# A strided v load on SyncE, old batches' rows loaded earlier, row scalings apart from their statistics, and a reordered block pair, in attention followed by LayerNorm and a feed-forward layer

## The chip, the cores and the metric

The kernel runs on one core of a Trainium2 chip. Its engines are TensorE (PE; PEld is its weight load), VectorE (DVE), ScalarE (ACT), GpSimd (POOL) and SyncE (SP), which issues transfers (DMAs); ScalarE issues some too. The metric is the device time of one execution in microseconds (us); lower is better.

## The reference

Eight batches of 576 tokens with eight heads of 64. Heads 0 to 3 see the last 32 tokens ("local"), heads 4 to 7 see the earlier tokens of the same residue modulo 32 ("strided"). The result, 512 wide, goes through a LayerNorm and a feed-forward layer of hidden width 2048, and is added to it.

```
rel = pos[:, None] - pos[None, :]
mask_local = (rel >= 0) & (rel < 32)
mask_strided = (rel >= 0) & (pos[None, :] % 32 == pos[:, None] % 32)
scores = where(mask, q @ k.T / 8, -1e9)          # local: heads 0..3, strided: heads 4..7
attn = exp(scores - max);  attn /= attn.sum() + 1e-9
x  = (attn @ v) as [batch, token, 512]
xn = (x - mean(x)) / sqrt(var(x) + 1e-6) * g_ln
out = x + relu(xn @ w_ch1) @ w_ch2
```

## The kernel before

**Tiling.** The feed-forward layer works on nine chunks of 512 tokens: chunk b is the first 512 tokens of batch b, and chunk 8 the last 64 tokens of all eight batches. The hidden width is cut into 16 blocks of 128. For each chunk and block, twelve products make `ph` (hidden before the relu; 4 slices of the model width by 3 products of high and low parts), ScalarE makes `hh` (relu, high part), VectorE makes `hl` (low part), and twelve products add the block to the output sums `po` (4 tiles of 128 tokens by 3). `ph` has one PSUM bank, so the `ph` of a block can begin only when the `hl` of the block before has been read out of it.

**Steps.** The main loop at lines 1359 to 1408 has one step for each chunk and block. A step issues `ph`, `hh` and `hl` of its own block, then the `po` products of the block before. Into the steps are woven: pieces of the attention (`visits`, a generator; heads are treated in pairs, two pairs of each kind to a batch), the weights' preparation, and the residual. TensorE, VectorE, ScalarE, POOL and SyncE each take their instructions in the order in which the program issues them. Attention results go to DRAM (`xdl` for local, `xds` for strided heads) and come back as rows.

**DMAs.** Every DMA that SyncE or ScalarE issues is given one of eight completion semaphores in turn, in the order of the program, and waits until the DMA eight places earlier, whichever engine issued it, has landed.

**The places that the change touches.** (1) `visits` loads the v of the pair two ahead (`load_v`, lines 404 to 419): for the last batches (`by_blocks`) through ScalarE's queue, six DMAs for a strided pair. (2) `coming` (line 1157) prepares, in the steps of chunk 6 (`runs[-1]`), what the last stage needs: the four row tiles of chunk 8 (`late["x8"]`), four row tiles of chunk 7 (two in `late["x"]`, named x, and two later ones, named xs), their normalisation and their transposes (`turn_last`, `turn_seventh`). Its time `at` is the step less 7; a half is the end of a step. (3) `x_normed` (line 785) takes the statistics of some tiles on VectorE, the reciprocal root on POOL, and multiplies the tiles on ScalarE. (4) The last stage, `two_steps` (line 1284), treats chunks 7 and 8 together, a pair of blocks at a time, with seven products of sums in place of eight; `u` and `v` are its PSUM sums, and between them stand the `po` products of the pair before (`waiting`). In the first pair those are the last block of chunk 6, whose output `prev[0].close()` adds to the residual (line 899) and stores.

Row tiles come from a pool of eight buffers (tag `tk`).

Of the kernel before, what the change touches and what calls it, by code (L numbers as in the profile page):

```python
# [12 lines left out]
AF = mybir.ActivationFunctionType  # L13
# [33 lines left out]
def kernel(  # L47
# [10 lines left out]
    nc = tc.nc  # L58

    B, H, S, D = q.shape  # L60
# [12 lines left out]
    NT = CH // P  # L73
# [49 lines left out]
    for jj in range(4):  # L123
        mrow = mask_l[STR * jj:STR * (jj + 1)]
        nc.gpsimd.affine_select(
            out=mrow, in_=mrow, pattern=[[1, 64]], base=-1,
            channel_multiplier=-1, compare_op=ALU.is_ge, fill=FILL)
        nc.gpsimd.affine_select(
            out=mrow, in_=mrow, pattern=[[-1, 64]], base=STR,
# [5 lines left out]
    for c in range(2):  # L135
        for r in range(3):
            msk = mask_s[64 * c:64 * (c + 1), NB * r:NB * (r + 1)]
            nc.gpsimd.affine_select(
                out=msk, in_=msk, pattern=[[-1, NB]], base=-NB * r,
# [619 lines left out]
    def x_load(c, i, t=None, halves=(0, 1)):  # L759

        if t is None:
            t = tkp.tile([P, DM], F32, tag="tk", name=f"x{c}_{i}")
        if c < B:
            parts = [(0, P, c, P * i)]
        else:
            parts = [(REST * j, REST, 2 * i + j, CH) for j in range(2)]
        for p0, n, b, r in parts:
            if 0 in halves:
                nc.sync.dma_start(t[p0:p0 + n, 0:DM // 2], xd_l[b][r:r + n, :])
            if 1 in halves:  # L770
                xs = xd_s[b][0:S].rearrange("(r t) d -> t r d", t=NB)
                nc.sync.dma_start(t[p0:p0 + n, DM // 2:DM], xs[r // STR:(r + n) // STR])
        return t
# [8 lines left out]
        nc.gpsimd.tensor_tensor(out=rs, in0=rs, in1=mhalf, op=ALU.pow)  # L782
        return rs

    def x_normed(name, xs):

        n = len(xs)
        mv = stp.tile([P, NT + 1, 2], F32, tag="mv5", name=f"mv{name}", bufs=1)
        rs = stp.tile([P, NT + 1], F32, tag="rs5", name=f"rs{name}", bufs=2)
        for i, x in enumerate(xs):  # L790
            st = stp.tile([P, 6], F32, tag="st", name=f"st{name}_{i}")
            nc.vector.bn_stats(st, x)
            nc.vector.bn_aggr(mv[:, i], st)
        nc.vector.tensor_scalar(rs[:, 0:n], mv[:, 0:n, 1], 1e-6, None, op0=ALU.add)
        nc.gpsimd.tensor_tensor(
            out=rs[:, 0:n], in0=rs[:, 0:n], in1=mhalf.broadcast_to([P, n]), op=ALU.pow)
        for i, x in enumerate(xs):
            nc.scalar.activation(out=x, in_=x, func=AF.Copy, scale=rs[:, i:i + 1])

    def x_turn(x, name):  # L800
        ps = fresh_bank(f"px{name}").rearrange("p (c x) -> p c x", c=NCC)
# [38 lines left out]
    def ffn2(run, f, h, tiles):  # L840
        for i in tiles:
            products(run.po[i], f, h, i, slice(0, DM), f == run.f0, f == run.f1 - 1)
# [173 lines left out]
    for step in ORDER.split():  # L1016
        what, x = step.split(".", 1)
        n0 = len(tc.nc.cur_bb.bb.instructions)
        if what[0] == "w":
            i = x[2:]  # L1020
# [40 lines left out]
    def visits():  # L1061

        for i in range(2 * NHP - 1, NP):
            p = pairs[i + 1] if i + 1 < NP else None
            pv = pairs[i] if i >= 2 * NHP else None
            scores_and_values(pv, p)
            by_blocks = i >= 3 * NHP
            px = pv if pv and pv.b + 1 < B else None
            if by_blocks:
                spread(px, p)  # L1070
            turned(i + 2)
            if by_blocks:
                yield
            if pv and i + 2 < NP:
                pairs[i + 2].load_v(queue=nc.scalar if by_blocks else nc.sync)
            yield
            (turn_blocks if by_blocks else weights_and_x)(px, p)
            if by_blocks and i + 3 < NP:
                pairs[i + 3].load_half(1, nc.scalar)
            yield  # L1080
# [50 lines left out]
    def turn_seventh(i):  # L1131

        cs = quarter[i]
        px = x_turn(late["x"][i], f"{B - 1}_{i}")
        xh, xl = (t[:, :, cs] for t in x_t(B - 1))
        t1, t2 = (late["ts"][i][:, n] for n in range(2))
        h, l = ([late[n + k][:, :, cs] for n in ("t1", "t2")] for k in "hl")
        nc.scalar.activation(out=xh, in_=px, func=AF.Copy)
        sub(nc.vector, t1, t1, px[:, 0:2])
        sub(nc.vector, t2, t2, t1)  # L1140
        nc.scalar.activation(out=h[0], in_=t1, func=AF.Copy)
        nc.scalar.activation(out=h[1], in_=t2, func=AF.Copy)
        sub(nc.vector, xl, px, raw(xh))
        sub(nc.vector, l[0], t1, raw(h[0]))
        sub(nc.vector, l[1], t2, raw(h[1]))
        sub(nc.vector, t1, t2, px[:, 0:2])
        sub(nc.vector, t2, px[:, 2:4], t2)
# [9 lines left out]
    def coming(f, end):  # L1157

        at = f + 0.5 * end - LAST

        def tiles(n, name):
            return [tkp.tile([P, DM], F32, tag="tk", name=f"{name}_{i}") for i in range(n)]

        if at == -4:
            late["x8"] = tiles(NT, f"x{B}")
            late["x"] = tiles(2, f"x{B - 1}")
        elif at in (-3.5, -2.5, -1.5):
            i = int(at + 3.5)
            x_load(B, i, late["x8"][i])
        elif at == -1:  # L1170
            for i, x in enumerate(late["x"]):
                x_load(B - 1, i + 2, x, (0,))
            x_load(B, NT - 1, late["x8"][NT - 1], (0,))
        elif at == -0.5:
            x_normed("a", late["x8"][0:3])
        elif at == 0.5:
            free_attention()
            x_load(B, NT - 1, late["x8"][NT - 1], (1,))
            for i, x in enumerate(late["x"]):
                x_load(B - 1, i, x, (0, 1) if i < 2 else (1,))  # L1180
        elif at == 2:
            turn_last(0)
            turn_last(1)
        elif at == 3:
            turn_last(2)
        elif at == 3.5:
            x_normed("b", late["x8"][3:] + late["x"])
        elif at == 5:
            turn_last(3)
            turn_seventh(0)  # L1190
        elif at == 5.5:
            turn_seventh(1)
        elif at == 6:
            turn_seventh(2)
            late["s"] = s_forms(0)
        elif at == 7:
            turn_seventh(3)
        elif at == 8:
            more_forms()
# [36 lines left out]
    def seven(po, w, x, start, stop=True):  # L1236

        wh, wl = (t.rearrange("p (c f) -> p c f", c=2) for t in w)
        xh, xl = x
        for c in range(2):  # L1240
            for k, (a, b) in enumerate(((wh, xh), (wh, xl), (wl, xh))):
                nc.tensor.matmul(po, a[:, c], b[:, c, :], start=(start and c + k == 0),  # L1242
                                 stop=(stop and c == 1 and k == 2), skip_group_check=True)
# [40 lines left out]
    def two_steps(p, s, waiting):  # L1284

        f0, f1 = 2 * p, 2 * p + 1
        a = weight_parts(p)
        s = [[x[:, 0], x[:, 1]] for x in s]
        xh, xl = x_t(B - 1)
        b11, b21 = ([t[:, k:k + 2] for t in (xh, xl)] for k in (0, 2))  # L1290
        t1, t2, b22 = ([late[n + k] for k in "hl"] for n in ("t1", "t2", "b22"))
        t3, t4 = ([late[n][:, k:k + 2] for k in (0, 2)] for n in ("t3", "t4"))
        c11 = fresh_bank(f"c11_{p}")
        seven(c11, a[0, 1], b21, True)
        u = fresh_bank(f"u_{p}")
        seven(u, a[0, 0], b11, True)
        p1 = kept(u, f"p1_{p}")
        if p + 1 < NFC // 2:
            coming_s = s_raws(p + 1)
        for work, tiles in waiting[:1]:  # L1300
            ffn2(*work, tiles)
        h0 = h_tiles(f"{B - 1}_{f0}")
        relu_sum(*h0, c11, p1)
        if not two:
            prev[0].close()
            two.append(Seventh())
        v = fresh_bank(f"v_{p}")
        seven(v, s[0], t1, True)
        seven(u, s[1], t2, False)
        p5 = kept(v, f"p5_{p}")  # L1310
        u2 = kept(u, f"u2_{p}")
        for work, tiles in waiting[1:]:
            ffn2(*work, tiles[:NT // 2])
        seven(u, s[2], t3, False)
        seven(v, s[3], b22, False)
        relu_sum(*h_late(f0, f1), u, p5)
        if p + 1 < NFC // 2:
            coming_s = s_parts(*coming_s)
        else:
            coming_s = None  # L1320
            two[0].load()
        for work, tiles in waiting[1:]:
            ffn2(*work, tiles[NT // 2:])
        seven(u, a[1, 1], t4, False)
        hh, hl = h_tiles(f"{B - 1}_{f1}")
        nc.scalar.activation(out=hh, in_=u, func=AF.Relu)
        nc.vector.scalar_tensor_tensor(
            out=hl, in0=u, scalar=0.0, in1=raw(hh), op0=ALU.max, op1=ALU.subtract)
        relu_sum(*h_late(f1, f0), v, u2)
        run = two[0].run  # L1330
        return coming_s, [((run, f0, h0), range(NT)), ((run, f1, (hh, hl)), range(NT))]
# [75 lines left out]
        prev = (r, f, h)  # L1407
        old, new = new, following
    forms = late["s"]
    waiting = [(prev, range(NT))]  # L1410
    fresh.append((ps_h, "h"))
    for p in range(NFC // 2):
        forms, waiting = two_steps(p, forms, waiting)
# [62 lines left out]
```

## Time and profile before

| | us |
|---|---|
| median of three runs | 910.92 (910.90, 910.92, 914.21) |
| profiled execution | 916.03, its span 914.2 |
| TensorE busy in the span | 885.7 (97%) |
| VectorE, ScalarE, POOL busy | 455.6, 241.8, 238.6 |
| TensorE busy in 0 to 60 us | 45.3 of 60 |
| in 60 to 600 us | 540.0 of 540 |
| in 600 to 640 / 640 to 680 us | 37.8 / 40.0 of 40 |
| in 680 to 700 / 700 to 720 us | 16.2 / 16.9 of 20 |
| in 720 to 760 / 760 to 914 us | 39.3 of 40 / 150.3 of 154 |
| granted TensorE clock, mean | 0.987 of full speed |

The span is the time from the first to the last instruction on the core. A busy TensorE is one that has a product in its pipeline, at whatever clock. The granted clock is a share of full speed: 0.5 and 1.0 are its two levels (1.2 and 2.4 GHz). An engine's waits are listed by what ended them; idle time of an engine on which nothing waits costs nothing.

### The profile page before, as it was taken

The page shows a single profiled execution, that of the slowest core. Times are in us where ns is not written, and L with a number is a line of the kernel's source. Part 1 is how long each engine was busy: PE and PEld are TensorE (multiplying, and loading weights), DVE is VectorE, ACT ScalarE, POOL GpSimd, SP SyncE. Part 2 cuts the span into 40 slices and gives each one's busy share as a digit, 9 for nine tenths or more (in the row PEclk, how much of TensorE's full clock was granted, in tenths as well). Part 3 has the DMA queues.
Part 4 walks back from the last instruction along what each step waited for, and adds up shares of the span by engine and source line. Part 5 has one row for each costly group of instructions (what it writes and reads, how often), then busy time and mean ns, then how long its engine had stood idle before and what let it go on. Part 6 is the DMA issues. An engine that isn't in the chain of part 4 may idle for free.

```text
span 914.2 us, 18339 instructions
## 1 busy us (share of the span) xinstructions
PE 885.7 (97%) x7431; PEld 725.0 (79%) x7431; DVE 455.6 (50%) x855; ACT 241.8 (26%) x433; POOL 238.6 (26%) x293
## 2 busy tenths in 40 slices
PE   6699999999999999999999999999998899999998
PEld 4578888888888888888888888887877678888886
DVE  5697475446754455545554464454642573332400
ACT  4566465112211111111111111111112344333200
POOL 6578287110100010001000010001000367676000
PEclk8899999999999999999999999999999999999999
DMA  9989791127795755666575658597732010001210
GB/s 207 204 188 264 168 281 35 21 50 175 141 172 113 125 103 133 120 119 110 117 132 107 121 102 153 110 150 114 143 89 77 7 63 1 1 0 37 81 45 24
DMA packets 330972, 100.64 MB, mean 110 GB/s; under 512 B 269712, under 2 KB 321800, under 8 KB 330888
## 3 DMA queue, kind: packets, MB, share of 16 engines
q1 hardware_dynamic: 258114, 86.11, 42.7%
q10 hardware_dynamic: 72774, 13.36, 9.8%
q8 instruction: 58, 0.95, 0.5%
q14 instruction: 26, 0.21, 0.1%
HBM read 72.37 MB, written 27.06 MB: 109 GB/s over the span
## 4 chain that ended last, share of the span: by engine, by line
PE 87%; issue 5%; DMA 3%; SPq 2%; ACT 2%; DVE 1%; POOL 0%; ACTq 0%; DVEq 0%; POOLq 0%
PE po L837 40%; PE ph L812 30%; PE u L1242 5%; PE sv L659 4%; PE v L1242 2%; PE c L1242 1%; SPq L722 1%; DMA x<-xds 1%; PE px L690 1%; DMA rows<-in_k_dram 1%; PE av L514 1%; PE pp L498 1%; PE av L523 0%; DMA sp<-wd 0%; PE t L377 0%
## 5 line engine op out<-in xcount | busy, mean ns | idle before, releaser
L837 PE MATMUL po<-w,hh 128*128 128x512 f32 x1024 | 320.6, 394 | 0.0
L812 PE MATMUL ph<-xh,w 128*128 128x512 f32 x880 | 294.3, 396 | 9.2 <-DVE hl L823 9.2
L837 PEld LDWEIGHTS po<-w,hh 128*128 128x128 f32 x1024 | 189.1, 188 | 39.6
L823 DVE SCALAR_TENSOR_TENSOR hl<-ph,hh 128x512 fp32r<-128x512 f32 x112 | 77.2, 690 | 282.4 <-ACT hh L818 282.4
L812 PEld LDWEIGHTS ph<-xh,w 128*128 128x128 f32 x880 | 167.4, 190 | 45.6 <-DVE hl L823 10.5
L837 PE MATMUL po<-w,hl 128*128 128x512 f32 x512 | 199.8, 390 | 0.0
L812 PE MATMUL ph<-xl,w 128*128 128x512 f32 x440 | 173.2, 394 | 0.0
L818 ACT ACTIVATE hh<-ph 128x512 fp32r<-128x512 f32 x112 | 66.8, 596 | 338.5 <-PE ph L812 259.7
L488 POOL TENSOR_TENSOR sm<-sm,mx 128x640 f32<-128x640 f32 (+1 forms) x32 | 40.6, 1270 | 350.0 <-issue 201.1
L837 PEld LDWEIGHTS po<-w,hl 128*128 128x128 f32 x512 | 96.1, 188 | 20.7
L812 PEld LDWEIGHTS ph<-xl,w 128*128 128x128 f32 x440 | 83.7, 190 | 17.0
L493 ACT ACTIVATE sm<-sm 128x640 f32<-128x640 f32 (+1 forms) x32 | 23.8, 743 | 104.8 <-POOL sm L488 104.8
L782 POOL TENSOR_TENSOR rs<-rs,mhalf 128x1 f32<-128x1 f32 x28 | 15.3, 550 | 125.2 <-DVE rs L781 90.3
L837 PE MATMUL po<-w,h 128*128 128x512 f32 x186 | 42.3, 389 | 0.0
L1114 POOL TENSOR_TENSOR sr<-sr,w 128x256 f32<-128x256 f32 x48 | 40.2, 838 | 3.8
L837 PEld LDWEIGHTS po<-w,h 128*128 128x128 f32 x186 | 34.9, 188 | 7.2
L1114 POOL TENSOR_TENSOR s<-sr,s 128x256 fp32r<-128x256 f32 x32 | 24.7, 801 | 26.6 <-ACT s L1228 26.6
L239 DVE SCALAR_TENSOR_TENSOR p<-s,p 128x512 uint32<-128x512 uint32 x32 | 22.0, 688 | 11.3 <-ACT p L235 11.2
L484 DVE TENSOR_REDUCE mx<-sm 128x10 f32<-128x640 f32 (+1 forms) x32 | 26.3, 822 | 1.9
L1114 DVE TENSOR_TENSOR x<-po,x 128x512 f32<-128x512 f32 x8 | 5.3, 688 | 39.6 <-PE po L837 29.9
L671 DVE TENSOR_TENSOR xo<-sv,den 128x256 f32<-128x256 f32 (+1 forms) x72 | 24.0, 389 | 0.0
L292 POOL TENSOR_TENSOR w<-r,w 128x512 fp32r<-128x512 f32 x16 | 20.6, 1294 | 8.4 <-ACT w L288 8.3
(193 smaller groups left out, 982.9 us busy)
## 6 DMA issues: line engine op xcount, KB each, us to landing
s<-in_moe_w_ch_dram SPq DMA_DIRECT2D x32, 512.0 KB
out_dram<-x SPq DMA_DIRECT2D x32, 256.0 KB
raw<-in_q_dram SPq DMA_DIRECT2D x104, 72.0 KB
raw<-in_k_dram ACTq DMA_DIRECT2D x68, 72.0 KB
x<-xdl SPq DMA_DIRECT2D x34, 128.0 KB
x<-xds SPq DMA_DIRECT2D x34, 128.0 KB
xdl<-xo SPq DMA_DIRECT2D x16, 256.0 KB
wd<-sm SPq DMA_DIRECT2D x10, 384.0 KB
```

The source lines that it names most:

```text
L239: nc.vector.scalar_tensor_tensor(out=self.p[i], in0=self.bits(i), scalar=3, in1=self.p[i], op0=ALU.logical_shift_left, op1=ALU.bitwise_or)
L484: engine(self.mx[:, :, 0:nt], self.smv, axis=AX.X)
L488: nc.gpsimd.tensor_tensor(out=sm, in0=sm, in1=mx[:, :, 0:nt].unsqueeze(3).broadcast_to([P, 2, nt, w]), op=ALU.subtract)
L493: nc.scalar.activation(out=self.smv, in_=self.smv, func=AF.Exp, scale=SCALE)
L659: nc.tensor.matmul(dst, at, by, start=True, stop=True, tile_position=pos)
L671: nc.vector.tensor_tensor(out=xot[0:n, :, t0:t1], in0=src, in1=pv.den[0:n, :, t0:t1].unsqueeze(3).broadcast_to([n, 2, t1 - t0, D]), op=ALU ...
L812: nc.tensor.matmul(ph, w[:, cc], x[:, cc, :], start=(n + k == 0), stop=(n == NCC - 1 and k == 2))
L818: nc.scalar.activation(out=hh, in_=ph, func=AF.Relu)
L823: nc.vector.scalar_tensor_tensor(out=hl, in0=ph, scalar=0.0, in1=hh.bitcast(F32), op0=ALU.max, op1=ALU.subtract)
L837: nc.tensor.matmul(po, hx[:, cs], w, start=(start and n == 0), stop=(stop and n == 2))
L1114: engine.tensor_tensor(out=out, in0=a, in1=b, op=op)
L1242: nc.tensor.matmul(po, a[:, c], b[:, c, :], start=(start and c + k == 0), stop=(stop and c == 1 and k == 2), skip_group_check=True)
```

## The change

Five edits:

- In one visit, that of pair 27 (`i == NP - 5`), the six v loads of pair 29 go through SyncE's queue instead of ScalarE's.
- The tiles of chunk 8 are taken, and the first three loaded, three steps earlier.
- `x_normed` is cut into `x_stats` (statistics and root) and `x_normed` (scalings). The statistics of the first three tiles move from the end of step 6 to the beginning of step 5, their scalings to the beginning of step 6.
- The statistics of the other five tiles stay at the end of step 10. Their scalings move from there: three to the end of step 11, two to the end of step 12.
- In the first pair of the last stage the `po` products of the last block of chunk 6 are cut in two halves, the second of which goes between the second and third use of `u`; `prev[0].close()` moves behind it, to the end of the pair.

```diff
@@ x_normed
-    def x_normed(name, xs):
+    def x_stats(name, xs):
...
-        for i, x in enumerate(xs):
-            nc.scalar.activation(out=x, in_=x, func=AF.Copy, scale=rs[:, i:i + 1])
+        return [(x, rs[:, i:i + 1]) for i, x in enumerate(xs)]
+
+    def x_normed(scaled):
+        for x, rs in scaled:
+            nc.scalar.activation(out=x, in_=x, func=AF.Copy, scale=rs)
@@ visits
-                pairs[i + 2].load_v(queue=nc.scalar if by_blocks else nc.sync)
+                pairs[i + 2].load_v(queue=nc.scalar if by_blocks and i != NP - 5 else nc.sync)
@@ coming
-        if at == -4:
+        if at == -7:
             late["x8"] = tiles(NT, f"x{B}")
+        elif at in (-6.5, -5.5, -4.5):
+            i = int(at + 6.5)
+            x_load(B, i, late["x8"][i])
+        elif at == -4:
             late["x"] = tiles(2, f"x{B - 1}")
-        elif at in (-3.5, -2.5, -1.5):
-            i = int(at + 3.5)
-            x_load(B, i, late["x8"][i])
+        elif at == -2:
+            late["a"] = x_stats("a", late["x8"][0:3])
         elif at == -1:
+            x_normed(late["a"])
...
-        elif at == -0.5:
-            x_normed("a", late["x8"][0:3])
...
         elif at == 3.5:
-            x_normed("b", late["x8"][3:] + late["x"])
+            late["b"] = x_stats("b", late["x8"][3:] + late["x"])
+        elif at == 4.5:
+            x_normed(late["b"][0:3])
...
         elif at == 5.5:
             turn_seventh(1)
+            x_normed(late["b"][3:])
@@ two_steps
-        if not two:
-            prev[0].close()
-            two.append(Seventh())
         v = fresh_bank(f"v_{p}")
...
         for work, tiles in waiting[1:]:
             ffn2(*work, tiles[NT // 2:])
+        if not two:
+            prev[0].close()
+            two.append(Seventh())
         seven(u, a[1, 1], t4, False)
@@ after the main loop
-    waiting = [(prev, range(NT))]
+    waiting = [(prev, range(NT // 2)), (prev, range(NT // 2, NT))]
```

Where the edits put the instructions is seen in the engines' orders. ScalarE in steps 12 to 14 of chunk 5, before (`v_s` is the v of a strided pair, `raw` holds a pair's q and k, `sx` a finished pair's rows):

```order
L818 ACTIVATE hh_12_6858<-ph_12_6845 128x512
L419 DMA v_s<-in_v_dram 18x11x64 x2
L419 DMA v_s<-in_v_dram 18x10x64
L419 DMA v_s<-in_v_dram 18x11x64 x2
L419 DMA v_s<-in_v_dram 18x10x64
L818 ACTIVATE hh_13_6900<-ph_13_6887 128x512
L729 ACTIVATE xh_6266<-sx_3_6823 128x512
L348 DMA raw_1_6864<-in_k_dram 32x18x32 x4
L818 ACTIVATE hh_14_6956<-ph_14_6943 128x512
```

ScalarE at the same place, now:

```order
L821 ACTIVATE hh_12_6858<-ph_12_6845 128x512
L821 ACTIVATE hh_13_6900<-ph_13_6887 128x512
L729 ACTIVATE xh_6266<-sx_3_6823 128x512
L348 DMA raw_1_6864<-in_k_dram 32x18x32 x4
L821 ACTIVATE hh_14_6956<-ph_14_6943 128x512
```

The loads of `v_s` have left ScalarE. On SyncE they now stand here, behind the `raw` of pair 30 and ahead of the next store of attention results:

```order
L722 DMA sp_0_6828<-wd_220 32x20x32 x4
L348 DMA raw_1_6864<-in_q_dram 32x18x32 x4
L419 DMA v_s<-in_v_dram 18x11x64 x2
L419 DMA v_s<-in_v_dram 18x10x64
L419 DMA v_s<-in_v_dram 18x11x64 x2
L419 DMA v_s<-in_v_dram 18x10x64
L548 DMA xdl_210<-xo_0_7025 128x4x128
```

VectorE in steps 5 to 7 of chunk 6, before (`sta` and `mva` are the statistics of the first three tiles, x_0 to x_2 of chunk 8):

```order
L823 SCALAR_TENSOR_TENSOR hl_5_7452<-ph_5_7437,hh_5_7450 128x512
L823 SCALAR_TENSOR_TENSOR hl_6_7485<-ph_6_7470,hh_6_7483 128x512
L569 TENSOR_REDUCE den_3_7487<-sm_199 128x12
L572 TENSOR_SCALAR den_3_7487<-den_3_7487 128x12
L573 RECIPROCAL den_3_7487<-den_3_7487 128x12
L737 STREAM_TRANSPOSE pt_3_7491<-sp_3_7416 128x768
L792 BN_STATS sta_7511<-x_0_7305 128x6
L793 BN_AGGR mva<-sta_7511 128x2
L792 BN_STATS sta_7514<-x_1_7306 128x6
L793 BN_AGGR mva<-sta_7514 128x2
L792 BN_STATS sta_7517<-x_2_7307 128x6
L793 BN_AGGR mva<-sta_7517 128x2
```

VectorE there, now:

```order
L826 SCALAR_TENSOR_TENSOR hl_5_7456<-ph_5_7441,hh_5_7454 128x512
L792 BN_STATS sta_7460<-x_0_7118 128x6
L793 BN_AGGR mva<-sta_7460 128x2
L792 BN_STATS sta_7463<-x_1_7119 128x6
L793 BN_AGGR mva<-sta_7463 128x2
L792 BN_STATS sta_7466<-x_2_7120 128x6
L793 BN_AGGR mva<-sta_7466 128x2
L794 TENSOR_SCALAR rsa<-mva 128x3
L826 SCALAR_TENSOR_TENSOR hl_6_7498<-ph_6_7483,hh_6_7496 128x512
L569 TENSOR_REDUCE den_3_7500<-sm_199 128x12
L572 TENSOR_SCALAR den_3_7500<-den_3_7500 128x12
L573 RECIPROCAL den_3_7500<-den_3_7500 128x12
```

The statistics and the sum for the root (`rsa`) have moved from behind the `hl` of step 6 and the attention's row sums to between the `hl` of steps 5 and 6.

ScalarE in steps 10 to 13 of chunk 6, before (`rsb` holds the five roots of the second set, x_3 of chunk 8 and xs, xs, x_0, x_1 of chunk 7; `b22h`, `xr`, `xh`, `t1h`, `t2h` are copies of turned tiles):

```order
L1128 COPY xr_7599<-px_2_7711 128x512
L798 ACTIVATE x_3_7308<-x_3_7308,rsb 128x512
L798 ACTIVATE xs_7607<-xs_7607,rsb 128x512
L798 ACTIVATE xs_7608<-xs_7608,rsb 128x512
L798 ACTIVATE x_0_7309<-x_0_7309,rsb 128x512
L798 ACTIVATE x_1_7310<-x_1_7310,rsb 128x512
L818 ACTIVATE hh_11_7768<-ph_11_7755 128x512
L818 ACTIVATE hh_12_7797<-ph_12_7784 128x512
```

ScalarE there, now:

```order
L1131 COPY xr_7599<-px_2_7711 128x512
L821 ACTIVATE hh_11_7763<-ph_11_7750 128x512
L801 ACTIVATE x_3_7121<-x_3_7121,rsb 128x512
L801 ACTIVATE xs_7607<-xs_7607,rsb 128x512
L801 ACTIVATE xs_7608<-xs_7608,rsb 128x512
L821 ACTIVATE hh_12_7795<-ph_12_7782 128x512
```

and some rows later, behind the turned tiles px_0 and px_1:

```order
L1141 ACTIVATE xh_7812<-px_1_7836 128x4x128
L1144 ACTIVATE t1h<-xr_7598 128x2x128
L1145 ACTIVATE t2h<-xr_7598 128x2x128
L801 ACTIVATE x_0_7321<-x_0_7321,rsb 128x512
L801 ACTIVATE x_1_7322<-x_1_7322,rsb 128x512
L821 ACTIVATE hh_13_7866<-ph_13_7853 128x512
```

Three of the five scalings have moved behind the `hh` of step 11, the other two behind the copies of two turned tiles, just ahead of the `hh` of step 13.

## Rows read from the trace of the kernel before

**Rows 1.** The page's busy line.

```profile
PE 885.7 (97%) x7431; PEld 725.0 (79%) x7431; DVE 455.6 (50%) x855; ACT 241.8 (26%) x433; POOL 238.6 (26%) x293
```

**Rows 2.** Waits of TensorE after 580 us: us in total, times, longest us.

```profile
PE ph L812 <- DVE hl L823: 9.2, 3, 3.8
...
PE u L1242 <- ACT u L1247: 0.7, 1, 0.7
```

**Rows 3.** Timeline of TensorE: start, duration, operation, [idle before and releaser].

```profile
621.93 0.79 PE L812 MATMUL ph<-xh,w 128*128 128x512 f32 x1 [2.25 <-DVE hl L823]
...
689.03 0.50 PE L812 MATMUL ph<-xh,w 128*128 128x512 f32 x1 [3.81 <-DVE hl L823]
...
693.42 0.69 PE L837 MATMUL po<-w,hh 128*128 128x512 f32 x2
...
717.23 0.65 PE L812 MATMUL ph<-xh,w 128*128 128x512 f32 x1 [3.14 <-DVE hl L823]
...
721.68 0.60 PE L803 MATMUL px<-ident,x 128*128 128x128 f32 x4
...
752.14 1.66 PE L1242 MATMUL u<-xh,s 128*128 128x512 f32 x6 [0.73 <-ACT u L1247]
...
753.64 0.40 PE L1242 MATMUL v<-b22h,s 128*128 128x512 f32 x1
```

**Rows 4.** Chain of waits, 590 to 640 us: start, duration, what.

```profile
593.33 3.13 DMA v_l<-in_v_dram
...
615.98 4.18 DMA sp<-wd
...
621.93 4.56 PE ph L812 x12
...
626.49 1.74 PE sv L659 x102
...
633.94 2.72 PE po L837 x12
```

**Rows 5.** Timeline of DMA issues on ScalarE's and SyncE's queues, 614 to 624 us.

```profile
614.91 5.54 ACTq L419 DMA_DIRECT2D v_s<-in_v_dram  x6
...
619.54 3.54 SPq L348 DMA_DIRECT2D raw<-in_q_dram  x4
```

**Rows 6.** Timeline of SyncE's issues, ScalarE and VectorE, 657 to 690 us.

```profile
657.46 0.49 SPq L769 DMA_DIRECT2D x<-xdl  x1
...
676.09 0.60 ACT L818 ACTIVATE hh<-ph 128x512 fp32r<-128x512 f32 x1 [4.84 <-PE ph L812]
...
683.74 0.69 DVE L792 BATCH_NORM_STATS2 sta<-x 128x6 f32<-128x512 f32 x1 [2.24 <-DMA x<-xds]
...
685.83 1.95 ACT L798 ACTIVATE x<-x,rsa 128x512 f32<-128x512 f32 x3 [9.14 <-POOL rsa L795]
```

**Rows 7.** Timeline of POOL and ScalarE, 711 to 717 us.

```profile
711.60 1.17 POOL L795 TENSOR_TENSOR rsb<-rsb,mhalf 128x5 f32<-128x5 f32 x1 [25.81 <-DVE rsb L794]
...
713.43 1.32 ACT L798 ACTIVATE xs<-xs,rsb 128x512 f32<-128x512 f32 x2
...
715.88 0.57 ACT L818 ACTIVATE hh<-ph 128x512 fp32r<-128x512 f32 x1
```

**Rows 8.** Timeline of ScalarE, TensorE and VectorE, 728 to 731 us.

```profile
728.33 0.42 ACT L1142 ACTIVATE t2h<-xr 128x256 fp32r<-128x256 f32 x1 [0.17 <-DVE xr L1114]
...
728.51 0.60 PE L803 MATMUL px<-ident,x 128*128 128x128 f32 x4
...
728.77 0.60 ACT L818 ACTIVATE hh<-ph 128x512 fp32r<-128x512 f32 x1
...
730.82 0.68 DVE L823 SCALAR_TENSOR_TENSOR hl<-ph,hh 128x512 fp32r<-128x512 f32 x1
```

**Rows 9.** Timeline of VectorE and ScalarE, 748 to 752 us.

```profile
748.87 2.71 DVE L899 SCALAR_TENSOR_TENSOR x<-po,rs,x 128x512 f32<-128x512 f32 x4
...
751.51 0.58 ACT L1247 COPY u<-u 128x512 f32<-128x512 f32 x1 [0.77 <-PE u L1242]
```

## Prediction, made before the result was known

> **What bounds the kernel now.** Read the page's busy line first: TensorE has 885.7 us of work in a span of 914.2 us [rows 1], the other engines are half idle. Only what lets TensorE wait less, or slows it, moves the time, and the most to be had is 28.5 us, part of it in the first 60 us, which the change leaves alone. Next, the list of TensorE's waits after 580 us: three waits of `ph` for VectorE's `hl`, together 9.2 us, and one of `u` for ScalarE, 0.7 us [rows 2]. Then the timeline, for where these four lie and what follows each [rows 3]: idle 2.25 us before 621.93, 3.81 before 689.03, 3.14 before 717.23, 0.73 before 752.14. After each of the first three, the twelve `ph` products take much longer than a normal group of twelve, 2.72 us: 4.56 us after the first [rows 4], 693.42 - 689.03 = 4.39 after the second, 721.68 - 717.23 = 4.45 after the third [rows 3]. TensorE runs at the lower clock level for a while after such a gap, and that belongs to the price of the wait. The short gap costs almost no clock: six products take 1.50 us (752.14 to 753.64) where half of 2.72 is 1.36.
>
> So the prices are A = 2.25 + 1.84 = 4.1, B = 3.81 + 1.67 = 5.5, C = 3.14 + 1.73 = 4.9 and D = 0.73 + 0.14 = 0.9 us. The change has an edit at each of the four.
>
> **A, the strided v through SyncE.** In step 12 of chunk 5, ScalarE's queue meets six v loads before the `hh` of step 13. They begin at 614.91 and need 5.54 us [rows 5], because they wait for earlier transfers: the chain of waits runs through a transfer `sp<-wd` that took 4.18 us to land [rows 4], until 620.16. `hh` follows the loads, `hl` follows `hh`, TensorE's `ph` of step 14 follows `hl`. With the loads on SyncE nothing stands there before `hh` of step 13, and all of A goes. What is added: on SyncE the six stand behind the `raw<-in_q` loads (issued from 619.54 for 3.54 us before [rows 5]), and ScalarE's own `raw<-in_k` loads, which come later in the program, can be held until the first v loads have landed. Suppose `sp<-wd` lands at 620.2 as before, the first v loads go out then and land 3.13 us later, as another v load did [rows 4], at 623.4: `hh` of step 14 then starts near 624 and `hl` is done 0.6 + 0.69 us later, at 625.3. TensorE, without its stall, ends the `ph` of step 14 near 621.93 - 2.25 + 2.72 = 622.4, and has 1.74 us of attention products and a group of 2.72 us [rows 4] before it wants that `hl`, at 626.9. So 1.5 us of cover is left. I take 4.1; the bounds are 0, where the wait passes to `raw<-in_k`, and 4.1.
>
> The Trainium skill, "DMA: Bandwidth & Descriptors", section "Issuing engines are not separate DMA queues", says that transfers started by either engine run on the same sixteen DMA engines, so that a second issuing engine saves only the time of the issue. In this trace the issuing engine did matter, since ScalarE's own work stood 5.54 us behind the loads. By the rule alone A would be worth next to nothing, and the sum 10.3 us.
>
> **B, the first three tiles of old batches loaded and measured earlier.** Their scalings stood on ScalarE until 685.83 because VectorE could begin the last tile's statistics only at 683.74 [rows 6], its loads being queued on SyncE behind the spreads. `hh` of step 7 waited behind the scalings. Now all three tiles are loaded one spread earlier: tile 0 went out from 657.46 [rows 6], tile 1 now goes about there and tile 2 some 2 us later, and a landing of 4 us leaves them there by 666. The statistics now stand ahead of `hl` of step 6, right behind that of step 5. `hh` of step 6 is at 676.09 [rows 6] and a step is two groups, 5.44 us, so `hl` of step 5 ends near 676.09 - 5.44 + 0.60 + 0.69 = 672. A tile's statistics take 0.69 us [rows 6] and a short aggregation, at most 1 us a tile, and the root at most the 1.17 us of five columns [rows 7]: done by 676.2. ScalarE is free for the scalings at 676.09 + 0.60; they take 1.95 us [rows 6], to 678.7, and `hh` of step 7 is due at 676.09 + 5.44 = 681.5. All of B goes: 5.5. Lower bound 1.5, if the loads come no earlier: then only the 2.2 us that VectorE stood for tile 2 and some of the queue shift.
>
> **C, the scalings of the second set.** Five scalings waited for POOL's root until 711.60 + 1.17 and held ScalarE until 715.88 [rows 7], with `hh` of step 11 behind them. Now this `hh` stands ahead. TensorE wanted the bank for step 12 at 717.23 - 3.14 = 714.1, and one group earlier, at 711.4, the `ph` of step 11 was complete. `hh` then takes 0.57 us [rows 7]; VectorE's statistics are done when the root begins, 711.6, so `hl` is done by 712.7, 1.4 us ahead. Three scalings of 0.66 us each (two take 1.32 [rows 7]) fill 712.8 to 714.8, and the next `hh` is due at 716.8. All of C goes: 4.9, with no transfer in it; bounds 4.5 and 4.9.
>
> **E, what C's edit adds.** The last two scalings now stand behind the `t2h` of the second turned tile, which begins at 728.33 and takes 0.42 us [rows 8]. TensorE wants the first of their tiles for its transposes at 728.51 [rows 8]. It gets it at 728.75 + 0.66 = 729.4 and waits 0.9 to 1.0 us. The pair pushes `hh` of step 13 from 728.77 to 730.1; but VectorE was busy until it began the `hl` of that step at 730.82 [rows 8], which hides it. The new wait is about as short as D's, so I add no clock: -1.0. Bounds -3.0 (with the clock of A to C) and 0.
>
> **D, the block pair.** Six `po` products are put between the second use of `u` and its third, so that the copy of `u` (751.51, 0.58 us [rows 9]) lies beside 1.36 us of products: 0.9 goes. The four closing adds, 2.71 us [rows 9], move behind the `h` of the same pair and delay the next `hl`, which is not wanted for more than 5 us. The banks that they free are wanted by the first products of the next run, five groups of six (6.8 us) after 751.3, at 758.1. The third use of `u` ends at 752.7, three elementwise steps of 0.6 to 0.7 us follow, then the adds: they end near 757.5. Cover 0.6 us. Bounds 0 and 0.9.
>
> **Sum.** 4.1 + 5.5 + 4.9 + 0.9 - 1.0 = 14.4 us. The profiled execution took 916.03 us (span 914.2, 1.8 around it) and would take 901.6. The median of the runs is 910.92, 5.1 us less, and one of the three was 914.21: something takes longer in the profiled execution. I take the whole 14.4 off the median: 896.5.
>
> **Rivals.** (1) A is not won: the wait passes to `raw<-in_k` and `hh` of step 14, or the median hardly had it, since A hangs on when one transfer lands. The 5.1 us between profile and median speak for the second (A is 4.1), the 1.5 us of cover against the first. (The Trainium skill's rule above would lead here.) Gain 14.4 - 4.1 = 10.3, time 900.6; if B too was shorter there by the 2.2 us of tile 2, 902.8. (2) Some of it returns in the last stage: E with the clock's price (2.0 more) and D not won (0.9). Gain 11.5, time 899.4. For it: only 0.6 us of cover in D. Against it: neither gap is as long as the shortest that cost clock. (3) The change does not do what it says in B: SyncE is held by the stores ahead of tile 0, and the tiles land as late as before. Gain 14.4 - 4.0 = 10.4, time 900.5. Against it: 6 us lie between landing and first use. (4) Slower: the v loads, waiting on SyncE, hold ScalarE at `raw<-in_k`, and `hh` of step 14 comes late by L. Beyond 1.5 us TensorE stands L - 1.5, and 1.8 more for the clock; that eats the 14.4 from L = 14.1 us on. At L = 16 the time is 910.9 - 14.4 + 16.3 = 912.8. That needs a landing near 637; the longest in these rows took 4.18 us.
>
> **How the numbers follow.** Forecast 62%, rival 1 20%, rival 2 9%, rival 3 7%, rival 4 2%. The forecast's own range is 894.5 to 898.5; rivals 1 to 3 reach 902.8. I give 893.8 to 902.8: the lower end has E at nothing and 1.7 us for the scatter of single runs. A measurement of this kernel can tell about 0.5%, 4.6 us, from no change, so faster means below 906.4. All cases but the last lie there; for doubt in a sum of small terms I put faster 0.93, within 0.5% 0.05, slower 0.02.
>
> **What would show it.** In the profile of the changed kernel: no wait of `ph` for `hl` over 0.3 us after 580 us; every `ph` group there between 2.7 and 3.0 us; a new wait of about 1 us of `px` for ScalarE near 714; no wait of `u` for its copy; a span near 900. The forecast is wrong if a gap above 1 us stands before the `ph` of step 14 or 15 of chunk 5, if the first three scalings still come after VectorE has stood for a tile's load, or if `po` waits for the closing adds.

## The result and the profile after

The changed kernel took 897.12 us (median of four runs, 895.68 to 899.14); the kernel before took 910.91 us beside it (910.19 to 914.21). The ratio is 0.9843, 95% interval [0.9812, 0.9874], that is 14.3 us less (11.5 to 17.1). The forecast was 896.5 us. The profiled execution took 896.80 us, its span 895.0. Two timed runs of the experiments, 3072.84 us in experiment 3 and 1460.34 us in the repeat of the changed kernel, were slow ones and are left out of the ratios below.

The page's busy line of the changed kernel, beside [rows 1]: TensorE's work has shrunk by 7.6 us with the same 7431 products, at a mean granted clock of 0.994 where it was 0.987; from 600 to 760 us, where the edits lie, it is now 1.00.

```profile
PE 878.1 (98%) x7431; PEld 721.1 (81%) x7431; DVE 455.5 (51%) x855; ACT 242.2 (27%) x433; POOL 238.7 (27%) x293
```

TensorE's waits after 580 us in the changed kernel, beside [rows 2] (us in total, times, longest): the four are gone and one new one, of `px`, stands there.

```profile
PE px L806 <- ACT x L801: 0.7, 1, 0.7
```

To see what each edit won, take TensorE's fixed points: products that stand at the same place of every version, on both sides of an edit. The distance between two of them holds a gap and the slower products behind it together. There are six. In the timeline of TensorE of the kernel before they are these (start, duration, operation), with the fifth, 721.68, in [rows 3] and the sixth, 728.51, in [rows 8]:

```profile
604.02 0.92 PE L659 MATMUL sv<-v_s,pt 54*64 54x64 f32 x44
626.42 0.97 PE L659 MATMUL sv<-v_l,pt 64*32 64x64 f32 x72
...
681.36 0.91 PE L659 MATMUL sv<-v_s,pt 54*64 54x64 f32 x44
698.95 1.03 PE L803 MATMUL px<-ident,x 128*128 128x128 f32 x8
```

The same in the changed kernel:

```profile
599.83 0.92 PE L659 MATMUL sv<-v_s,pt 54*64 54x64 f32 x44
618.11 0.97 PE L659 MATMUL sv<-v_l,pt 64*32 64x64 f32 x72
...
672.96 0.92 PE L659 MATMUL sv<-v_s,pt 54*64 54x64 f32 x44
684.83 1.03 PE L806 MATMUL px<-ident,x 128*128 128x128 f32 x8
...
702.54 0.60 PE L806 MATMUL px<-ident,x 128*128 128x128 f32 x4
...
710.27 0.66 PE L806 MATMUL px<-ident,x 128*128 128x128 f32 x4 [0.75 <-ACT x L801]
```

The distances between neighbours, in us, for all profiled executions that the text speaks of; each is the difference of two such starts, the last one that of the span and the start of the sixth point. "Start" is the time to the first point, and the stretch between the second and third point is "rest":

| kernel | start | A | rest | B | C | E | to the end (D) |
|---|---|---|---|---|---|---|---|
| before | 604.02 | 22.40 | 54.94 | 17.59 | 22.73 | 6.83 | 185.69 |
| changed | 599.83 | 18.28 | 54.85 | 11.87 | 17.71 | 7.73 | 184.73 |
| changed, again | 598.87 | 18.28 | 54.85 | 11.87 | 17.71 | 7.73 | 184.69 |
| v alone | 601.44 | 18.29 | 54.85 | 17.28 | 22.72 | 6.85 | 185.67 |
| rows alone | 599.96 | 22.40 | 54.87 | 11.87 | 23.57 | 7.17 | 185.76 |
| scalings alone | 602.57 | 22.47 | 55.01 | 18.62 | 17.71 | 7.74 | 185.78 |
| block pair alone | 603.25 | 21.17 | 54.93 | 17.24 | 22.73 | 6.86 | 184.62 |
| five together | 601.58 | 18.29 | 54.84 | 11.87 | 17.71 | 6.83 | 184.68 |
| loads only | 599.60 | 18.28 | 54.85 | 13.28 | 17.71 | 7.73 | 184.75 |
| v one hh later | 602.78 | 20.20 | 56.49 | 11.87 | 17.71 | 7.73 | 184.72 |
| v behind the copy | 601.14 | 18.29 | 55.03 | 11.86 | 17.71 | 7.73 | 184.74 |

From before to after: A 4.12, B 5.72, C 5.02, E -0.90, D 0.96, the rest 0.09, together 15.0. The spans differ by 19.2; the other 4.2 lie in "start", ahead of every edit.

### The profile page after: what moved, and what is told of

Read it like the earlier page. It is cut to its first block, busy times and chain, and to the rows that moved or that the text cites. A ratio compares the mean times of both kernels' runs of the same rounds, so it can differ in the third digit from the quotient of the medians.

```text
span 895.0 us, 18342 instructions
## 1 busy us (share of the span) xinstructions
PE 878.1 (98%) x7431; PEld 721.1 (81%) x7431; DVE 455.5 (51%) x855; ACT 242.2 (27%) x433; POOL 238.7 (27%) x293
## 4 chain that ended last, share of the span: by engine, by line
PE 95%; ACT 1%; DVE 1%; DMA 1%; issue 1%; SPq 0%; POOL 0%; POOLq 0%; ACTq 0%
PE po L840 44%; PE ph L815 33%; PE u L1250 5%; PE sv L659 5%; PE v L1250 2%; PE c L1250 1%; PE px L690 1%; DMA rows<-in_k_dram 1%; PE pp L498 1%; PE av L514 0%; PE cm L270 0%; PE t L377 0%; PE ph L970 0%; PE px L559 0%; PE sp L457 0%
## 5 line engine op out<-in xcount | busy, mean ns | idle before, releaser
L815 PE MATMUL ph<-xh,w 128*128 128x512 f32 x880 | 290.4, 391 | 0.0
L815 PEld LDWEIGHTS ph<-xh,w 128*128 128x128 f32 x880 | 165.2, 188 | 34.2
L815 PE MATMUL ph<-xl,w 128*128 128x512 f32 x440 | 171.2, 389 | 0.0
L1117 DVE TENSOR_TENSOR p<-u,p 128x512 f32<-128x512 f32 x8 | 5.5, 692 | 34.1 <-PE u L1250 34.1
```

Of the source, the lines that this page charges most:

```text
L815: nc.tensor.matmul(ph, w[:, cc], x[:, cc, :], start=(n + k == 0), stop=(n == NCC - 1 and k == 2))
L1117: engine.tensor_tensor(out=out, in0=a, in1=b, op=op)
```

## What each edit does in the profile after

**A.** The rows around step 13 of chunk 5 in the changed kernel (a queue's row gives the time of the issue; [..] is idle time before and its releaser):

```profile
612.84 0.60 ACT L821 ACTIVATE hh<-ph 128x512 fp32r<-128x512 f32 x1 [4.84 <-PE ph L815]
613.01 2.07 SPq L348 DMA_DIRECT2D raw<-in_q_dram  x4
...
615.12 2.42 SPq L419 DMA_DIRECT2D v_s<-in_v_dram  x6
...
616.61 1.97 ACTq L348 DMA_DIRECT2D raw<-in_k_dram  x4
...
618.68 0.60 ACT L821 ACTIVATE hh<-ph 128x512 fp32r<-128x512 f32 x1 [3.23 <-DMA raw<-in_k_dram]
...
619.31 0.69 DVE L826 SCALAR_TENSOR_TENSOR hl<-ph,hh 128x512 fp32r<-128x512 f32 x1
...
622.70 0.39 PE L815 MATMUL ph<-xh,w 128*128 128x512 f32 x1
```

The `hh` of step 13 (612.84) has nothing ahead of it. The wait that the prediction feared is there, but small: `raw<-in_k` holds the `hh` of step 14 until 618.68. The `hl` of that step ends at 620.00, and TensorE wants the bank at 622.70, the start of the next `ph`: 2.7 us of cover where the prediction counted 1.5. The six loads need 2.42 us on SyncE, where they needed 5.54 on ScalarE [rows 5]: on SyncE they do not stand for the spread.

**B.** VectorE, POOL and ScalarE in steps 5 to 7 of chunk 6 of the changed kernel, beside [rows 6]:

```profile
663.49 0.68 DVE L792 BATCH_NORM_STATS2 sta<-x 128x6 f32<-128x512 f32 x1
...
666.48 0.86 POOL L795 TENSOR_TENSOR rsa<-rsa,mhalf 128x3 f32<-128x3 f32 x1 [6.72 <-DVE rsa L794]
667.69 0.60 ACT L821 ACTIVATE hh<-ph 128x512 fp32r<-128x512 f32 x1 [4.84 <-PE ph L815]
668.18 1.94 ACT L801 ACTIVATE x<-x,rsa 128x512 f32<-128x512 f32 x3
...
673.13 0.60 ACT L821 ACTIVATE hh<-ph 128x512 fp32r<-128x512 f32 x1 [3.00 <-PE ph L815]
```

VectorE waits for no tile, the root is ready 0.35 us before the `hh` of step 6 and the scalings fit behind it, with 3.0 us to spare before the `hh` of step 7.

**C and E.** ScalarE around steps 11 to 13 of chunk 6, beside [rows 7, 8]:

```profile
697.29 0.60 ACT L821 ACTIVATE hh<-ph 128x512 fp32r<-128x512 f32 x1 [4.58 <-PE ph L815]
...
698.68 0.72 ACT L801 ACTIVATE x<-x,rsb 128x512 f32<-128x512 f32 x1 [0.79 <-POOL rsb L795]
...
699.31 1.32 ACT L801 ACTIVATE xs<-xs,rsb 128x512 f32<-128x512 f32 x2
702.79 0.60 ACT L821 ACTIVATE hh<-ph 128x512 fp32r<-128x512 f32 x1 [2.17 <-PE ph L815]
...
709.18 0.42 ACT L1145 ACTIVATE t2h<-xr 128x256 fp32r<-128x256 f32 x1 [0.17 <-DVE xr L1117]
709.51 1.32 ACT L801 ACTIVATE x<-x,rsb 128x512 f32<-128x512 f32 x2
```

The `hh` of step 11 goes first (697.29) and three scalings follow the root, 2.2 us ahead of the `hh` of step 12. The last two stand behind `t2h`, and TensorE's `px` waits 0.75 us for the first of them.

**D.** TensorE and VectorE in the first block pair of the last stage of the changed kernel:

```profile
733.07 1.52 PE L1250 MATMUL u<-xh,s 128*128 128x512 f32 x6
...
736.70 2.72 DVE L902 SCALAR_TENSOR_TENSOR x<-po,rs,x 128x512 f32<-128x512 f32 x4
...
739.87 0.62 PE L840 MATMUL po<-w,hh 128*128 128x512 f32 x2
```

The third use of `u` has no wait, where [rows 3] had 0.73 us. The closing adds end at 739.42 and the banks are wanted at 739.87: 0.45 us of cover, where the prediction counted 0.6.

## Experiments

The first four each do one part alone, on the kernel before, which took 912.56 us in that series (23 runs).

**1. The v through SyncE alone.** Edit: the one line in `visits`.

> The kernel before with one edit, the six v loads of pair 29 on SyncE. If ScalarE's queue was what held hh of step 13 (my theory), the gap before ph of step 14 in chunk 5 goes and the two attention visits around it lie 18.3 us apart instead of 22.4: 4.1 us less in the profile, and in the timed runs too if they had the gap. If the transfers themselves were late (rival: the wait passes to raw<-in_k and hh of step 14), the visits stay 21 us or more apart and the time is within 1 us of before. If the wait was a thing of the profiled execution only (second rival), the profile shows 18.3 us but the timed difference is under 1.5 us.

Measured: ratio 0.9955 [0.9941, 0.9969], -4.1 us. In its table row A is 18.29, as in the changed kernel; of the other stretches behind "start" none is more than 0.31 us from that of before. So A is in the medians too, and both halves of rival 1 fall, that the wait passes on and that the median hardly had it.

**2. The rows of old batches alone.** Edit: loads, statistics and scalings of the first three tiles as in the change; the second set and all else as before.

> The kernel before with the earlier loads of the first three tiles and their statistics and scalings moved, nothing else. Theory: the gap before ph of step 8 in chunk 6 goes with its lower clock, 5.5 to 5.7 us less from the last attention visit to the first transposes; the other three gaps stay. Rival (the tiles land as late as before): 1.5 us less, with VectorE standing for a tile's load before the hl of step 6. Timed: 5.5 against 1.5 us less.

Measured: ratio 0.9930 [0.9911, 0.9949], -6.4 us; B is 11.87. Rival 3 (the tiles land as late as before) falls.

**3. The scalings of the second set alone.**

```diff
-            x_normed("b", late["x8"][3:] + late["x"])
+            late["b"] = x_stats("b", late["x8"][3:] + late["x"])
+        elif at == 4.5:
+            x_normed(late["b"][0:3])
...
             turn_seventh(1)
+            x_normed(late["b"][3:])
```

> The kernel before with the five scalings of the second set issued apart from their statistics, nothing else. Theory: the gap before ph of step 12 goes (4.9 to 5.0 us less) and a new wait of px for the scaling of x appears in step 13, 0.75 to 1.0 us: net 4.0 us less. If the new wait costs clock as the long gaps do, net 2 us less.

Measured: ratio 0.9968 [0.9953, 0.9984], -2.9 us (1.5 to 4.3). C is 17.71, and E is 7.74 where it was 6.83: the new wait comes with this edit, and costs 0.9.

**4. The block pair alone.** Edit: `waiting` in two halves and `prev[0].close()` at the end of the pair.

> The kernel before with the first pair of the last stage reordered, nothing else. Theory: the wait of u for its copy (0.73 us) goes, no wait of po for the closing adds comes, and the stretch from the last ph to the end is 0.9 to 1.0 us shorter in the profile; the timed difference is too small to tell. Rival (closing adds late): a wait of po for VectorE of 0.3 us or more in the second pair, the stretch no shorter.

Measured: ratio 0.9998 [0.9985, 1.0011], -0.2 us (-1.4 to +1.0). The time can't tell it from nothing; in the profile the wait of `u` is gone and the last stretch is 1.07 us shorter (184.62).

The four add up to -13.6 us, all together gave -14.3. In the table, too, each stretch with its edit alone is within 0.11 us of that of the changed kernel: nothing shows that the edits lean on each other.

**5. All five scalings behind the `hh` of step 11,** in the changed kernel. This and the next three are versions of the changed kernel; it ran again beside 5, 6 and 7:

> The changed kernel once more, beside the other kernels of this series. Theory: 897 us, 13.5 to 14.5 us below the kernel before. Rival, that the 14.3 us was partly the luck of a few runs: 12 us or less.

Measured: ratio 0.9851 [0.9828, 0.9874], -13.6 us (11.5 to 15.7); its table row is that of the first profile to 0.04 us, but for "start".

```diff
-            x_normed(late["b"][0:3])
+            x_normed(late["b"])
...
-            x_normed(late["b"][3:])
```

> The changed kernel, with all five scalings of the second set behind the hh of step 11 of chunk 6 (two of them stood behind the copies of the turned tiles, at the end of step 12). Theory: the new wait of px for the scaling of x_0 (0.75 us, and some 0.2 us around it) comes only from these two scalings standing behind the copies; the five take 3.3 us on ScalarE, and the next hh is due about 4 us after the first begins, so the wait goes and nothing takes its place: 0.7 to 1.0 us less than the changed kernel, near 896.2. Rival: the five together hold the hh of step 12 and with it a ph by some tenths of a us, and the px wait is only traded for a ph wait: the same time as the changed kernel or up to 2 us more.

Measured: 895.27 us, ratio 0.9814 [0.9796, 0.9833]. The intervals of the two ratios overlap, but the profile is clear. ScalarE and TensorE of this version:

```profile
702.29 1.32 ACT L801 ACTIVATE x<-x,rsb 128x512 f32<-128x512 f32 x2
...
704.55 0.60 ACT L821 ACTIVATE hh<-ph 128x512 fp32r<-128x512 f32 x1 [0.94 <-PE ph L815]
...
711.12 0.60 PE L806 MATMUL px<-ident,x 128*128 128x128 f32 x4
```

The fifth scaling ends 0.94 us before the next `hh` can start, `px` has no wait, TensorE has no wait at all after 560 us, and E is back to 6.83: 0.90 us won in the profile. This version has the lowest median of the case, but the times alone do not set it apart from the changed kernel.

**6. The loads early, statistics and scalings where they were.**

```diff
-        elif at == -2:
-            late["a"] = x_stats("a", late["x8"][0:3])
         elif at == -1:
-            x_normed(late["a"])
...
+        elif at == -0.5:
+            x_normed(x_stats("a", late["x8"][0:3]))
```

> The changed kernel, with the statistics and scalings of the first three tiles of chunk 8 back at the end of step 6 of chunk 6; their loads stay three steps early. Theory: the loads alone take away only VectorE's stand for the last tile (2.2 us) and part of the shift; the statistics still stand behind the hl of step 6 and the attention's row sums, and the three scalings ahead of the hh of step 7, so about 1 us of a wait of ph is left before the ph of step 8, with some lower clock behind it: 1.2 to 3 us slower than the changed kernel, 898 to 900. Rival: the early loads are all of it, and the statistics' place does not matter: the changed kernel's time within 0.5 us.

Measured: 898.16 us, ratio 0.9847 [0.9829, 0.9865]; B is 13.28, 1.41 more than in the changed kernel. The times do not show this difference (the ratio of the changed kernel beside it was 0.9851), so what follows rests on the profile. VectorE, POOL, ScalarE and TensorE there:

```profile
672.46 0.66 DVE L792 BATCH_NORM_STATS2 sta<-x 128x6 f32<-128x512 f32 x1
...
673.61 0.86 POOL L795 TENSOR_TENSOR rsa<-rsa,mhalf 128x3 f32<-128x3 f32 x1 [14.08 <-DVE rsa L794]
674.51 1.95 ACT L801 ACTIVATE x<-x,rsa 128x512 f32<-128x512 f32 x3 [6.45 <-POOL rsa L795]
676.36 0.57 ACT L821 ACTIVATE hh<-ph 128x512 fp32r<-128x512 f32 x1
...
677.71 0.50 PE L815 MATMUL ph<-xh,w 128*128 128x512 f32 x1 [1.12 <-DVE hl L826]
```

With the tiles there, VectorE does its statistics without a stop, but root and scalings still stand ahead of the `hh` of step 7. Of B's 5.7 us the early loads give 4.3 and, with them in place, the earlier statistics and scalings 1.4.

**7. The v loads back on ScalarE, behind the `hh` of step 13.**

```diff
-            if pv and i + 2 < NP:
-                pairs[i + 2].load_v(queue=nc.scalar if by_blocks and i != NP - 5 else nc.sync)
+            if pv and i + 2 < NP and i != NP - 5:
+                pairs[i + 2].load_v(queue=nc.scalar if by_blocks else nc.sync)
             yield
+            if i == NP - 5:
+                pairs[i + 2].load_v(queue=nc.scalar)
             (turn_blocks if by_blocks else weights_and_x)(px, p)
```

> The changed kernel, with the six v loads of pair 29 back on ScalarE's queue, but issued one step later, behind the hh of step 13 of chunk 5 and ahead of the raw<-in_k loads. Theory: the gap came from the place of the loads in ScalarE's order, ahead of that hh while a spread had not yet landed; which engine issues them does not matter by itself. Behind the hh they find the spread landed, they are issued in some 2.5 us, and the hh of step 14 keeps its time: no gap over 0.3 us, the changed kernel's time within 1 us. Rival: only the other engine's queue helps, since ScalarE can not issue ten loads and stay in time: a gap of 1 us or more before the ph of step 15 and 2 to 4 us more time than the changed kernel.

Measured: 901.26 us, ratio 0.9883 [0.9864, 0.9903]; A is 20.20, 1.9 more than in the changed kernel, and the rest is 1.6 longer. By the ratios it is 2.9 us slower than the changed kernel beside it, as the rival said, but neither theory had the gaps where they are. Timeline of all engines:

```profile
613.88 2.09 SPq L722 DMA_DIRECT2D sp<-wd  x4
...
616.06 2.07 SPq L348 DMA_DIRECT2D raw<-in_q_dram  x4
...
616.34 3.92 ACTq L419 DMA_DIRECT2D v_s<-in_v_dram  x6
...
620.39 0.63 ACT L729 ACTIVATE xh<-sx 128x512 fp32r<-128x512 f32 x1 [4.00 <-DMA raw<-in_q_dram]
...
621.05 0.69 DVE L733 TENSOR_TENSOR xl<-sx,xh 128x512 fp32r<-128x512 f32 x1 [2.62 <-ACT xh L729]
...
622.04 0.84 DVE L737 STREAM_TRANSPOSE pt<-sp 128x640 f32<-128x640 f32 x1
...
622.98 0.96 PE L659 MATMUL sv<-v_l,pt 64*32 64x64 f32 x72 [1.85 <-issue]
...
648.85 7.92 ACTq L419 DMA_DIRECT2D v_s<-in_v_dram  x6
...
653.55 1.96 SPq L722 DMA_DIRECT2D sp<-wd  x4
...
656.87 0.60 ACT L821 ACTIVATE hh<-ph 128x512 fp32r<-128x512 f32 x1 [7.45 <-DMA v_s<-in_v_dram]
...
658.25 0.50 PE L815 MATMUL ph<-xh,w 128*128 128x512 f32 x1 [1.36 <-DVE hl L826]
```

Read it upward from the gap of 1.85 us, which the profile calls "issue" without a releaser: `sv` needs `pt`, which ends at 622.88; `pt` stands behind `xl` on VectorE; `xl` needs `xh`; and `xh` stands behind the six loads on ScalarE. The theory's step that failed is that the loads would find the spread landed. By the semaphore numbers in the trace the first four have those of the spread `sp<-wd` (613.88) and the last two those of the first two `raw<-in_q` (616.06), and each goes out 2.4 to 3.4 us after the DMA that has the same one. So a delay of transfers passes through ScalarE and VectorE to TensorE. The second gap is a knock-on: with the order of the DMAs shifted, the v loads of pair 31 (648.85, 7.92 us; in the changed kernel 4.97) got other completion semaphores in turn and had to wait for a spread `sp<-wd` that was only issued at 653.55 (the fourth load has the semaphore of its first one), and the `hh` behind them with it; the chain of waits runs from the landing of that spread to the loads. It is A's stall once more, at another pair.

**8. The same loads on ScalarE, behind the copy `xh`.** Edit: as in 7, with the two added lines behind `turn_blocks`. There the loads of pair 31 have the same waits as in the changed kernel.

> The changed kernel, with the six v loads of pair 29 on ScalarE's queue once more, now behind the copy xh<-sx of the same step and ahead of the raw<-in_k loads (in the run before they stood ahead of that copy). Theory: what cost 1.85 us there was the order on ScalarE, the copy behind the loads, VectorE's xl behind the copy, the transpose pt behind xl and TensorE's products sv behind pt. With the copy ahead of the loads this chain is free of them; the hh of step 14 still comes behind the raw<-in_k loads near 1.9 us after its ph and is covered by a group of twelve and the sv products; the second gap of that run (1.36 us, the v loads of pair 31 behind a spread) goes too, since these again wait for the transfers they wait for in the changed kernel. No gap, visits 18.3 us apart, the changed kernel's time within 1 us: ScalarE may issue the loads, if what others wait for stands ahead of them. Rival, that the other engine's queue is itself needed: the sv gap or one before the ph of step 15 of 1 us or more stays, 2 us or more over the changed kernel.

Measured: 897.28 us, ratio 0.9828 [0.9791, 0.9864], the changed kernel's time. Timeline:

```profile
614.34 2.07 SPq L348 DMA_DIRECT2D raw<-in_q_dram  x4
...
616.13 0.63 ACT L729 ACTIVATE xh<-sx 128x512 fp32r<-128x512 f32 x1 [1.38 <-DVE sx L727]
616.14 2.34 ACTq L419 DMA_DIRECT2D v_s<-in_v_dram  x6
...
618.52 2.00 ACTq L348 DMA_DIRECT2D raw<-in_k_dram  x4
...
619.43 0.97 PE L659 MATMUL sv<-v_l,pt 64*32 64x64 f32 x72
...
620.61 0.60 ACT L821 ACTIVATE hh<-ph 128x512 fp32r<-128x512 f32 x1 [3.85 <-DMA raw<-in_k_dram]
```

No gap, with all ten loads on ScalarE. The six have the same semaphores as in 7, but begin 1.8 us behind the first `raw<-in_q` (616.14 and 614.34) where they began 0.3 us behind it (616.34 and 616.06), and go out in 2.34 us. What had cost A was the place of the loads in an in-order queue, ahead of work that others waited for and at a time when their turn's semaphore was not yet free; the other engine is one way out of it, a later place another.

## Why the prediction was right

- **A, forecast 4.1: 4.12.** The mechanism held, experiments 1 and 8 show it. Only the cover was sized too small (1.5 against 2.7 us), on the safe side, since the loads did not stand for the spread on SyncE. The Trainium skill, "DMA: Bandwidth & Descriptors", section "Issuing engines are not separate DMA queues", gave next to nothing for A as the prediction applied it. Experiment 8 agrees with what it says of the transfers, since the issuing engine made no difference by itself (897.28 against 897.12 us). The 4.1 us were those of the instructions queued behind the issue.
- **B, forecast 5.5: 5.72.** The lower bound of 1.5, for loads that come no earlier, was not needed. Of the two halves of the edit the loads carried more (experiment 6).
- **C, forecast 4.9: 5.02.** With 2.2 us left before the next `hh`, against 2.0 forecast.
- **E, forecast -1.0: -0.90,** 0.75 of it the wait. No clock was lost behind it, as assumed (granted 1.00 from 710.20 to 720.20): rival 2's first half falls. Experiment 5 shows that E was avoidable.
- **D, forecast 0.9: 0.96 in the profile.** The run times of experiment 4 do not show so little; the narrow cover of the closing adds held, and with it rival 2's second half falls.
- **Sum, forecast 14.4: 14.3 in the medians, 13.6 in the repeat, 15.0 in the table.** The five terms were right one by one; that the median came within 0.6 us of the forecast is in part luck, since the nine runs of the changed kernel that count lie between 895.68 and 901.01 us. Rival 4 fails on its size: behind `raw<-in_k` the `hh` of step 14 starts 0.4 us later than one step after that of step 13 (618.68 against 612.84 + 5.44), not 14.
- **The 5.1 us between profile and median.** The prediction took this for a sign that a stall, perhaps A, was longer in the profiled execution. The runs give other reasons. The profile's five prices (14.9 us) agree with the medians' 14.3. The execution was long in its first stretch: "start" is 604.02, 2.9 us above the mean of the other ten rows of the table. And the median of three was low: the same kernel's medians beside the experiments are 912.56, 912.64 and 912.36 us. So no long stall is needed for it. The doubt that rival 1 drew from it was not baseless all the same, since the profile of experiment 4 has A at 2.9 us; but experiment 1 shows it at 4.1 (2.8 to 5.4) in the medians. The sign "a span near 900" missed (895.0): 4.2 us of the difference to before are the shorter first stretch, which no edit touches.

## What to carry to other kernels

An engine that both computes and issues DMAs passes each DMA's wait on to the work behind it: read the issue's own duration (5.54 us against 2.4 us for the same six loads), and move either the loads or the work, whichever is easier. Price a stall between two fixed points of the bounding engine, not by its idle time alone, and compare edits by those distances, stretch by stretch, when the run times scatter by more than an edit is worth. After moving a DMA where semaphores are dealt in turn, look at the next DMAs of the same kind, since they may now wait for something else.

## What was not expected of the hardware

The price of one and the same gap differs between executions. A's gap cost 4.12 us in the kernel before, and in the block pair alone, with a gap as long (2.31 against 2.25 us), only 2.9 (21.17 - 18.28). The windows of ten us behind the gap show why (us, TensorE, its weight loads, VectorE, ScalarE and POOL busy, then the granted clock, the DMA share and GB/s). In the kernel before:

```profile
621.90:631.90 10.00, 9.97 (x144) 8.00 (x145) 8.19 (x19) 1.59 (x3) 2.37 (x3) 0.83 0.35 58
```

In the block pair alone:

```profile
621.20:631.20 10.00, 9.79 (x150) 7.94 (x151) 8.01 (x19) 1.99 (x3) 2.37 (x3) 1.00 0.41 79
```

The one was at the lower clock level for part of the window (0.83), the other stayed at full speed. What decides between the two, these runs do not tell. B's price lay between 5.4 and 6.8 us by the table (17.24 and 18.62 less 11.87; its idle time between 3.47 and 3.81), C's between 5.0 and 5.9. The shorter gaps cost little beyond themselves: behind the 0.75 us of E, the 1.12 us of experiment 6 and the 1.36 and 1.85 us of experiment 7 the granted clock of the next ten us was 1.00, and they cost 0.90, 1.41, 1.64 and 1.92 us. And the first stretch, which no edit touches, scatters by 5.2 us over these profiles (598.87 to 604.02), about as much as the largest edit is worth.
